# Laying out the output projection of seven heads as four rows per partition in a decode kernel

## The chip, the cores and the metric

The kernel runs on one core of a Trainium2 chip. The metric is the device time of one execution in microseconds; lower is better. Before and after were always timed in alternating rounds on the same chip.

Two numbers are given for every run: the *time* (the metric) and the *span*, which goes from the first instruction of the trace to the last.

## The reference, cut to what matters

One decode token passes through two branches that a sigmoid gate mixes. The attention branch has 16 query heads, 8 KV heads, 65536 cached positions and head size 256, so it reads 512 MiB of K and V. Its result goes through `wo`, 4096 x 448 in bf16 (3.67 MB).

```python
q = (x @ wq).reshape(B, Sq, 16, 256).transpose(0, 2, 1, 3)
k, v = repeat(k_cache, 2, axis=1), repeat(v_cache, 2, axis=1)
p = softmax(einsum("bhqd,bhkd->bhqk", q, k) * 256 ** -0.5)
o = einsum("bhqk,bhkd->bhqd", p, v)
a = o.transpose(0, 2, 1, 3).reshape(B, Sq, 16 * 256) @ wo      # wo: 4096 x 448
out = g * a + (1 - g) * b                                      # b: a small gated MLP
```

Of the kernel before, what the change touches and what calls it, by code (L numbers as in the profile page):

```python
# [12 lines left out]
ALU = AluOpType  # L13
# [11 lines left out]
class _Plan:  # L25
# [8 lines left out]
    def op(self, eng, key, fn, deps=()):  # L34
        o = _Op(eng, key, fn, deps)
        self.ops.append(o)
        return o

    def dma(self, eng, key, sem, fn, deps=()):
        if sem not in self.dsem:  # L40
            self.dsem[sem] = self.es.enter_context(self.nc.semaphore("d_" + sem))
        o = _Op(eng, key, fn, deps, dma=sem)
        self.ops.append(o)
        return o
# [75 lines left out]
def bass_gated_mix__gqa_block_cached__glu_gated_reglu__decode_kernel(  # L120
# [13 lines left out]
    H = A_k_cache.shape[1]  # L134
    S = A_k_cache.shape[2]
    DH = A_k_cache.shape[3]
    D = A_x.shape[2]
    F = B_W_gate.shape[1]
    NQ = A_wq.shape[1]
    J = 2 * H  # L140
# [15 lines left out]
    with es:  # L156
# [3 lines left out]
        ring = [sb("ring%d" % i, [128, U * DH], BF) for i in range(NRING)]  # L160
# [8 lines left out]
        o_sb = sb("o_sb", [128, 512], BF)  # L169
# [7 lines left out]
        emat = sb("emat", [128, 4], BF)  # L177
# [4 lines left out]
        X = sb("hs", [128, 20], F32)  # L182
        attnT = sb("attnT", [128, H * 4], BF)
# [32 lines left out]
        T_ps = M_ps[:, 480:484]  # L216
# [5 lines left out]
        op, dma = pl.op, pl.dma  # L222
        touch_m = []

        def mop(*a, **k):
            o = op(*a, **k)
            touch_m.append(o)
            return o
# [17 lines left out]
        t = 3.0  # L246
# [10 lines left out]
        slot, held, freed = {}, {2: ["gu", "dn"]}, {}  # L257
        r = 0
        for kind, i, _ in order:
            if kind in ("k", "v") or (kind, i) in (("wo", 0), ("vp", 0)):  # L260
# [3 lines left out]
                held[sl] = [(kind, i)]  # L264
                r += 1
        wo_sb = ring[slot["wo", 0]][:, 0:J * 2 * D].rearrange("p (j s n) -> p j s n", j=J, s=2)


        d_x = dma("ac", -9, "x", lambda e: e.dma_start(x_row, A_x[0, :, :]))
# [25 lines left out]
        g_em = op("gp", 0.4, lambda e: e.tensor_scalar(emat[:], iot1[:], 0.0, None, ALU.is_equal), [prev])  # L295
# [63 lines left out]
        def v_src(i):  # L359
            h, a = divmod(i, NTH)  # L360
            return A_v_cache[0, h, a * TK:(a + 1) * TK, :].rearrange("(m u) d -> m (u d)", u=U)
# [25 lines left out]
        def proj(e, lhsT, rhs, start, stop):  # L387
            for g in range(2):
                ins = e.matmul(A_ps[32 * g:32 * g + 1, 0:D2], lhsT, rhs[:, g * D2:(g + 1) * D2], start=start, stop=stop,  # L389
                               skip_group_check=True, tile_position=(0, 32 * g))  # L390
            return ins

        l_, qk, smax, aexp, pv, last = {}, {}, {}, {}, {}, {}
        pending = []

        def free(key):
            out_ = []
            for f in freed[key]:
                out_.append(l_[f] if isinstance(f, str) else qk[f[1], 1] if f[0] == "k" else pv[f[1]])
            return out_  # L400

        def make_pv(n, lo, hi, sl, tv, dep):
            h, a = divmod(n, NTH)

            def f_pv(e):
                for k in range(lo // 2, hi // 2):
                    g = k % 4
                    col = k * 16 + a
                    ins = e.matmul(OP[32 * g:32 * g + 4, :], ptp[:, col:col + 13:4],  # L409
                                   ring[sl][:, k * 512:(k + 1) * 512],  # L410
                                   start=(a == 0 and k < 4), stop=(a == NTH - 1 and k >= U // 2 - 4),
                                   tile_position=(0, 32 * g))
                return ins
            tp = max(tv, last["tev", h])
            deps = [dep] + last["ev", h] + ([last.get(("ocp", h - 1)), c_ps[2]] if a == 0 else [])
            pv[n] = op("pe", tp, f_pv, deps)
            if a == NTH - 1 and hi == U:
                tn = tp + (8.0 if n < NT - 1 else 1.2)
                o1 = op("dv", tn, lambda e: e.tensor_copy(o_sb[:], OP[:]), [pv[n], last.get(("otr", h - 1))])  # L419

                def f_otr(e):
                    for s in range(2):
                        for par in range(2):
                            ins = e.matmul(T_ps[:, 2 * s:2 * s + 2], o_sb[:, par * 256 + s:par * 256 + 256:2],  # L424
                                           emat[:, 2 * par:2 * par + 2], start=(par == 0), stop=(par == 1))
                    return ins
                o2 = mop("pe", tn + 0.5, f_otr, [o1, g_em])
                o3 = mop("dv", tn + 1, lambda e: e.tensor_tensor(
                    attnT[:, h * 4:(h + 1) * 4].rearrange("p (s q) -> p s q", q=2),
                    T_ps.rearrange("p (s q) -> p s q", q=2),  # L430
                    X[:, 8:10].unsqueeze(1).to_broadcast([128, 2, 2]), ALU.mult), [o2, last["rc", h]])
                last["ocp", h], last["otr", h], last["norm", h] = o1, o2, o3
                last["tn", h] = tn + 1

        for kind, i, t in issue:
# [43 lines left out]
            elif kind == "k":  # L479
                n = i  # L480
                h, t_ = divmod(n, NTH)
# [15 lines left out]
                if t_ == NTH - 1:  # L497
# [12 lines left out]
                    for rd in range(2):  # L510
# [10 lines left out]
                        p = op("pe", tt + 0.5, f_ptr, [rsc, g_idb, last.get(("bank", rd))])  # L521
# [7 lines left out]
                        q = op("ac", tt + 1, f_ev, [p, pv.get(h * NTH - 1)])  # L529
# [13 lines left out]
                    for args in [p_ for p_ in pending if p_[0] // NTH == h]:  # L543
                        make_pv(*args)
                        pending.remove(args)
            elif kind in ("v", "vp"):
                if kind == "v":
                    n, lo, hi = i, 0, U
                    sl = slot["v", n]
                    dep = dma("sp", t, "r%d" % sl, lambda e, sl=sl, n=n: e.dma_start(ring[sl][:], v_src(n)), free(("v", n)))  # L550
                else:
                    n, (lo, hi) = NT - 1, PIECES[i]
                    sl = slot["vp", 0]
                    dep = dma("sp", t, "vp%d" % i, lambda e, sl=sl, n=n, lo=lo, hi=hi: e.dma_start(  # L554
                        ring[sl][:, lo * 256:hi * 256], v_src(n)[:, lo * 256:hi * 256]), free(("vp", 0)))
                args = (n, lo, hi, sl, tL[kind, i], dep)
                if ("tev", n // NTH) in last:
                    make_pv(*args)
                else:
                    pending.append(args)  # L560
            elif kind == "wo":
                lo, hi = WO[i]
                l_["wo", i] = dma("sp", t, "wo%d" % i, lambda e, lo=lo, hi=hi: e.dma_start(
                    wo_sb[:, lo:hi, :, :], A_wo[lo * 256:hi * 256, :].rearrange("(j p s) n -> p j s n", p=128, s=2)), free(("wo", 0)))

        LAST = last["tn", H - 1]
        for i, (lo, hi) in enumerate(WO):
            for h in range(lo // 2, (hi + 1) // 2):
                key = max(tL["v", NT - 3] + 8, last["tn", h] + 0.5) + 0.01 * h
                if i in (1, 2):  # L570
                    key = LAST - (0.7, 0.2)[i - 1]
                elif i > 2:
                    key = LAST + 2 + 0.1 * i

                def f_wo(e, h=h, lo=max(lo, 2 * h), hi=min(hi, 2 * h + 2)):
                    for j in range(lo, hi):
                        for s in range(2):
                            c = h * 4 + s * 2 + j - 2 * h
                            ins = proj(e, attnT[:, c:c + 1], wo_sb[:, j, s, :], False, j == J - 1 and s == 1)
                    return ins  # L580
                fin = op("pe", key, f_wo, [l_["wo", i], last["norm", h], l_["dn"]])
        f0 = op("dv", T_END, lambda e: e.tensor_copy(fin_o[:, 0:D2], A_ps[0:1, 0:D2]), [fin])  # L582
        f1 = op("ac", T_END, lambda e: e.copy(fin_o[:, D2:D], A_ps[32:33, 0:D2]), [fin])
        f2 = dma("sp", T_END + 1, "out", lambda e: e.dma_start(out[0, :, :], fin_o), [f0, f1])
# [3 lines left out]
        pe = progs["pe"]  # L588
# [54 lines left out]
```

## The kernel before: what the change and the argument touch

All loads stand on one DMA queue. K and V come in tiles of 8 MiB (64 KiB per partition) into three ring buffers. The stream ends in this order: last K tile, V tile, first `wo` transfer (heads 0 to 4, 2240 KB), two V tiles (the second one in five pieces), then `wo` in four small transfers (448, 448, 224, 224 KB). These small ones fill the time in which the last V piece still has to be multiplied, copied and transposed.

```python
NW = H - 3
order += [("wo", 0, 7.3), ("v", NT - 3, TILE), ("v", NT - 2, TILE)]
PIECES = [(0, 64), (64, 96), (96, 112), (112, 120), (120, 128)]
...
WO = [(0, 2 * NW), (2 * NW, J - 4), (J - 4, J - 2), (J - 2, J - 1), (J - 1, J)]
```

A half head of `wo` (256 rows, index `j`) lies as two consecutive rows per partition, so every piece that a DMA moves is 2 x 448 x 2 = 1792 bytes. The attention output of a KV head (two query heads side by side in `o_sb`) must stand in the same order. Four small matmuls transpose it and one VectorE instruction scales it:

```python
def f_otr(e):
    for s in range(2):
        for par in range(2):
            ins = e.matmul(T_ps[:, 2 * s:2 * s + 2], o_sb[:, par * 256 + s:par * 256 + 256:2],
                           emat[:, 2 * par:2 * par + 2], start=(par == 0), stop=(par == 1))
    return ins
o2 = mop("pe", tn + 0.5, f_otr, [o1, g_em])
o3 = mop("dv", tn + 1, lambda e: e.tensor_tensor(attnT[...], T_ps..., X[:, 8:10]..., ALU.mult), ...)
...
l_["wo", i] = dma("sp", t, "wo%d" % i, lambda e, lo=lo, hi=hi: e.dma_start(
    wo_sb[:, lo:hi, :, :], A_wo[lo * 256:hi * 256, :].rearrange("(j p s) n -> p j s n", p=128, s=2)), free(("wo", 0)))
```

TensorE runs most of its program in a loop over the KV heads; what follows the loop (the last V tiles and the projection) is straight code.

## Time and profile before

| | before |
|---|---|
| time, median of 3 runs (range) | 1277.79 us (1277.51 to 1278.08) |
| span of the profiled run | 1276.2 us |
| DMA | 549.03 MB, mean 430 GB/s |
| TensorE / VectorE / ScalarE busy | 33% / 50% / 5% |

The DMA lines of the page show 40 equal slices of the span. The digit is the busy share in tenths, the second line the rate; the third counts packets by size:

```profile
DMA  9999999999999999999999999999999999999998
GB/s 398 443 433 430 435 429 438 435 431 429 435 433 440 428 429 435 433 440 429 431 435 431 438 431 433 435 431 432 438 431 431 435 431 438 433 429 435 415 444 348
DMA packets 12948, 549.22 MB, mean 430 GB/s; under 512 B 1283, under 2 KB 3590, under 8 KB 3974
```

No slice shows a pause. Between the first slice and the last, the slowest is the one with the small packets of the first `wo` transfer: it reads 415 GB/s. The last lines of the chain of waits (start, duration, what) show how the kernel ends:

```profile
1239.27 32.48 DMA ring<-in_A_wo_dram
1271.74 0.04 issue
1271.79 0.91 PE A_ps L389 x8
1272.70 0.20 PE M_ps L424 x4
1272.90 0.01 issue
1272.91 1.68 PE A_ps L389 x16
1274.59 0.02 issue
1274.61 0.38 DVE P_sb L582
```

TensorE waits until 1271.74 us for a `wo` transfer, then projects, transposes the last head (line 424) and projects the rest. The last four projections in turn wait for the last `wo` transfer, which lands at 1273.92 us, so this landing sets the end:

```profile
1273.96 0.15 PEld L389 LDWEIGHTS A_ps<-ring,attnT 128*1 128x1 bf16 x4 [0.22 <-DMA ring<-in_A_wo_dram]
```

Two issue lines matter as well. The first `wo` transfer was issued at 1173.78 us and landed 38.3 us later, at 1212.1 us. The V tile behind it was issued only at 1208.11 us, when the scores of the last K tile had freed its buffer:

```profile
ring<-in_A_wo_dram SPq DMA_DIRECT2D x1, 2240.0 KB, 38.3
```

```profile
1208.11 0.34 SPq L550 DMA_DIRECT2D ring<-in_A_v_cache_dram  x1
```

One more reading is needed, which no table of the profile shows. Each DMA is spread over 16 DMA engines, and its semaphore is raised once by each engine. The semaphore records of the trace therefore give 16 landing times for every transfer. For the first `wo` transfer they run from 1209.23 to 1212.10 us: the leading engine is 2.87 us ahead of the slowest. The transfer before it landed last at 1206.25 us, so the first `wo` transfer costs the slowest engine 5.85 us. "Lands" below means the last of the 16.

### The profile page before, as it was taken

How to read it: one execution, taken by the hardware profiler on the slowest of the kernel's cores; microseconds unless marked ns; L12 is line 12 of the kernel's file. 1: busy time of each engine (PE TensorE's matmuls, PEld its weight loads, DVE VectorE, ACT ScalarE, POOL GpSimd, SP SyncE). 2: the span in 40 equal slices, each digit the busy share in tenths (PEclk: the TensorE clock that was granted, in tenths of full speed). 3: DMA queues.
4: the chain of work that ended last, by engine and by line, in shares of the span. 5: the costliest groups of instructions: out<-in, count | busy, mean ns of one | idle time of the engine just before them, and what ended most of it. 6: DMA issues, size and time to landing. Idle time of an engine off the chain costs nothing. (4 is left out here: it accounts for less than half of the span.)

```text
span 1276.2 us, 10216 instructions
## 1 busy us (share of the span) xinstructions
PE 426.9 (33%) x4568; PEld 167.3 (13%) x4568; DVE 633.4 (50%) x421; ACT 63.3 (5%) x124; POOL 4.1 (0%) x21
## 2 busy tenths in 40 slices
PE   3633322334223431224331343321333313233255
PEld 1501110111001210002110111100111101011021
DVE  2698633465433655434555444555434655335600
ACT  0000000010000100001000010000100001000000
POOL 1000000000000000000000000000000000000000
PEclk9656666656666565666656666656666656666565
DMA  9999999999999999999999999999999999999998
GB/s 398 443 433 430 435 429 438 435 431 429 435 433 440 428 429 435 433 440 429 431 435 431 438 431 433 435 431 432 438 431 431 435 431 438 433 429 435 415 444 348
DMA packets 12948, 549.22 MB, mean 430 GB/s; under 512 B 1283, under 2 KB 3590, under 8 KB 3974
## 3 DMA queue, kind: packets, MB, share of 16 engines
q1 hardware_dynamic: 12930, 549.03, 99.7%
q8 instruction: 8, 0.13, 0.0%
q14 instruction: 6, 0.05, 0.0%
q10 hardware_dynamic: 4, 0.00, 0.0%
HBM read 549.03 MB, written 0.00 MB: 430 GB/s over the span
## 5 line engine op out<-in xcount | busy, mean ns | idle before, releaser
L367 DVE STREAM_TRANSPOSE ring<-ring 128x2048 uint32<-128x2048 uint32 x256 | 565.4, 2275 | 396.5 <-DMA ring<-in_A_k_cache_dram 396.5
L378 PE MATMUL ST<-ring,xc 128*16 128x512 bf16 x2048 | 223.9, 611 | 745.6 <-PEq L86 745.6
L378 PEld LDWEIGHTS ST<-ring,xc 128*16 128x16 bf16 x2048 | 68.3, 120 | 887.0 <-issue 886.1
L409 PE MATMUL O<-ring,ptp 128*4 128x512 bf16 x2048 | 150.7, 457 | 32.7 <-DMA ring<-in_A_v_cache_dram 18.7
L494 ACT ACTIVATE P_sb<-ST,nmb 128x512 bf16<-128x512 f32 x32 | 45.1, 1410 | 1102.2 <-DVE nmb L492 1102.2
L492 DVE TENSOR_REDUCE nmb<-ST 128x1 f32<-128x512 f32 x32 | 22.0, 689 | 116.8 <-PE ST L378 116.8
L409 PEld LDWEIGHTS O<-ring,ptp 128*4 128x4 bf16 x2048 | 56.4, 99 | 126.6 <-issue 69.3
L419 DVE CAST o_sb<-O 128x512 bf16<-128x512 f32 x8 | 5.5, 691 | 78.6 <-PE O L409 78.6
L513 DVE TENSOR_TENSOR P_sb<-P_sb,hs 128x1024 bf16<-128x1024 bf16 x16 | 18.9, 1221 | 9.4 <-ACT hs L507 9.4
L518 PE MATMUL PT<-identb,P_sb 128*128 128x128 bf16 x128 | 16.2, 307 | 16.8 <-PEq L86 15.8
L459 PE MATMUL M_ps<-xT,ring 128*128 128x1 bf16 x84 | 9.5, 205 | 17.2 <-DMA ring<-in_B_W_up_dram 17.2
L518 PEld LDWEIGHTS PT<-identb,P_sb 128*128 128x128 bf16 x128 | 12.4, 138 | 19.2 <-issue 19.2
L527 ACT COPY ptp<-PT 128x256 bf16<-128x256 bf16 x32 | 10.3, 375 | 23.9 <-PE PT L518 23.9
L341 PE MATMUL QN<-ring,P_sb 128*128 128x512 bf16 x32 | 8.9, 448 | 3.1 <-DMA ring<-in_A_wq_dram 3.1
L459 PEld LDWEIGHTS M_ps<-xT,ring 128*128 128x128 bf16 x84 | 7.2, 152 | 17.8 <-issue 17.4
L494 ACT ACTIVATION_READ_ACCUMULATOR P_sb<-ST,nmb 128x1 f32 x32 | 8.4, 262 | 0.0
L462 PE MATMUL M_ps<-xT,ring 128*64 128x1 bf16 x56 | 7.8, 276 | 0.0
L442 DVE STREAM_TRANSPOSE scr<-P_sb 128x256 uint32<-128x256 uint32 x1 | 0.4, 445 | 12.5 <-ACT P_sb L441 12.5
L503 PE MATMUL M_ps<-identf,hs 128*2 128x128 f32 x8 | 2.5, 308 | 11.1 <-PEq L86 11.1
L539 DVE RECIPROCAL hs<-M_ps 128x2 f32<-128x2 f32 x8 | 1.4, 170 | 8.3 <-PE M_ps L538 8.3
L462 PEld LDWEIGHTS M_ps<-xT,ring 128*64 128x64 bf16 x56 | 5.4, 191 | 0.4
L389 PE MATMUL A_ps<-ring,attnT 128*1 128x224 bf16 x64 | 4.6, 306 | 0.7 <-DMA ring<-in_A_wo_dram 0.6
(74 smaller groups left out, 65.7 us busy)
## 6 DMA issues: line engine op xcount, KB each, us to landing
ring<-in_A_v_cache_dram SPq DMA_DIRECT2D x1, 4096.0 KB, 23.6
ring<-in_A_wq_dram SPq DMA_DIRECT2D x1, 3072.0 KB, 10.5
ring<-in_A_wo_dram SPq DMA_DIRECT2D x1, 2240.0 KB, 38.3
ring<-in_A_v_cache_dram SPq DMA_DIRECT2D x1, 2048.0 KB, 28.2
ring<-in_B_W_down_dram SPq DMA_DIRECT2D x1, 1568.0 KB, 21.7
ring<-in_B_W_gate_dram SPq DMA_DIRECT2D x1, 1344.0 KB, 32.9
ring<-in_B_W_up_dram SPq DMA_DIRECT2D x1, 1344.0 KB, 35.5
ring<-in_A_v_cache_dram SPq DMA_DIRECT2D x1, 1024.0 KB, 30.2
```

The source lines that it names most:

```text
L341: ins = e.matmul(QN_ps, xw3[:, k_, 31 - h:159 - h], rhs, start=(h == 0 and kt == 0), stop=(h == H - 1 and kt == R3))
L367: return lambda e: e.transpose(v, v)
L378: ins = e.matmul(bank[32 * w:32 * w + 16, :], xc[:, x0:x0 + 16], ktv[sl][:, u0:u0 + 16, c, :, r_], start=(b == 0 and c == 0 and r_ == 0), ...
L409: ins = e.matmul(OP[32 * g:32 * g + 4, :], ptp[:, col:col + 13:4], ring[sl][:, k * 512:(k + 1) * 512], start=(a == 0 and k < 4), stop=(a = ...
L419: o1 = op("dv", tn, lambda e: e.tensor_copy(o_sb[:], OP[:]), [pv[n], last.get(("otr", h - 1))])
L459: e.matmul(GU_ps[:, c:c + 1], wf3[which][:, kt * F + ft:(kt + 1) * F:FT], xT[:, kt:kt + 1], start=(kt == 0), stop=False, skip_group_check= ...
L462: ins = e.matmul(GU_ps[64 * half:64 * half + 64, c:c + 1], wfh[which][:, ft:F // 2:FT], xT[:, R3 + half:R3 + half + 1], start=False, stop= ...
L492: smax[n] = op("dv", tk + 22, lambda e, n=n, NM=NM, t_=t_: e.tensor_reduce(NM[:, t_:t_ + 1], ST[n % 2][:], AX.X, ALU.max, negate=True), [q ...
L494: aexp[n] = op("ac", tk + 23, lambda e, n=n, t_=t_, NM=NM, RS=RS: e.activation(P_sb[:, t_:2048:4], ST[n % 2][:], ACTF.Exp, bias=NM[:, t_:t ...
L513: rsc = op("dv", tt, lambda e, X=X, pb=pb: e.tensor_tensor(pb, pb, X[:, 12:16].unsqueeze(1).to_broadcast([128, 256, 4]), ALU.mult), [h7, a ...
L518: ins = e.transpose(PT[rd][:, s * 128:(s + 1) * 128], P_sb[:, (rd * 8 + s) * 128:(rd * 8 + s + 1) * 128], identb[:, :])
L527: ins = e.copy(dst, src)
```

## The change: intent and diff

The intent is to halve the number of DMA pieces of `wo` without moving more bytes: four rows per partition make pieces of 3584 B. A whole KV head (512 rows) then is one piece per partition. Head 7 is left alone, because it comes in halves at the very end. In exchange the transposition needs 16 smaller matmuls per head instead of four, and the scaling two VectorE instructions instead of one.

```diff
+        wo4 = ring[slot["wo", 0]][:, 0:J * 2 * D].rearrange("p (h s n) -> p h s n", h=H, s=4)
...
+                def f_otr4(e):
+                    for s in range(4):
+                        for q in range(2):
+                            for par in range(2):
+                                ins = e.matmul(T_ps[64 * q:64 * q + 64, s:s + 1], o_sb[:, par * 256 + s:par * 256 + 256:4],
+                                               emat[:, 2 * par + q:2 * par + q + 1], start=(par == 0), stop=(par == 1),
+                                               skip_group_check=True)
+                    return ins
+
+                def f_norm4(e):
+                    for q in range(2):
+                        ins = e.tensor_scalar(attnT[64 * q:64 * q + 64, h * 4:(h + 1) * 4], T_ps[64 * q:64 * q + 64, :],
+                                              X[64 * q:64 * q + 64, 8 + q:9 + q], None, ALU.mult)
+                    return ins
...                                                        # both for h < H - 1
+                if hi <= J - 2:
+                    dst, src = wo4[:, lo // 2:hi // 2, :, :], A_wo[lo * 256:hi * 256, :].rearrange("(h p s) n -> p h s n", p=128, s=4)
+                else:
+                    dst, src = wo_sb[:, lo:hi, :, :], A_wo[lo * 256:hi * 256, :].rearrange("(j p s) n -> p j s n", p=128, s=2)
...                                                        # and f_wo4, the projection from the new order
```

More of the change, by code (lines that the diff above doesn't have):

```diff
@@ L426, in f_otr @@
                     return ins
-                o2 = mop("pe", tn + 0.5, f_otr, [o1, g_em])
-                o3 = mop("dv", tn + 1, lambda e: e.tensor_tensor(
+                def f_otr4(e):
[11 more added lines that the diff above has]
+                    return ins
+                o2 = mop("pe", tn + 0.5, f_otr if h == H - 1 else f_otr4, [o1, g_em])
+                o3 = mop("dv", tn + 1, f_norm4 if h < H - 1 else lambda e: e.tensor_tensor(
                     attnT[:, h * 4:(h + 1) * 4].rearrange("p (s q) -> p s q", q=2),
@@ L562, in bass_gated_mix__gqa_block_cached__glu_gated_reglu__decode_kernel @@
                 lo, hi = WO[i]
-                l_["wo", i] = dma("sp", t, "wo%d" % i, lambda e, lo=lo, hi=hi: e.dma_start(
-                    wo_sb[:, lo:hi, :, :], A_wo[lo * 256:hi * 256, :].rearrange("(j p s) n -> p j s n", p=128, s=2)), free(("wo", 0)))
+                if hi <= J - 2:
+                    dst, src = wo4[:, lo // 2:hi // 2, :, :], A_wo[lo * 256:hi * 256, :].rearrange("(h p s) n -> p h s n", p=128, s=4)
+                else:
+                    dst, src = wo_sb[:, lo:hi, :, :], A_wo[lo * 256:hi * 256, :].rearrange("(j p s) n -> p j s n", p=128, s=2)
+                l_["wo", i] = dma("sp", t, "wo%d" % i, lambda e, dst=dst, src=src: e.dma_start(dst, src), free(("wo", 0)))
         LAST = last["tn", H - 1]
@@ L573, in bass_gated_mix__gqa_block_cached__glu_gated_reglu__decode_kernel, with f_wo4 @@
                     key = LAST + 2 + 0.1 * i
+                def f_wo4(e, h=h):
+                    for s in range(4):
+                        ins = proj(e, attnT[:, h * 4 + s:h * 4 + s + 1], wo4[:, h, s, :], False, False)
+                    return ins
                 def f_wo(e, h=h, lo=max(lo, 2 * h), hi=min(hi, 2 * h + 2)):
@@ L580, in f_wo @@
                     return ins
-                fin = op("pe", key, f_wo, [l_["wo", i], last["norm", h], l_["dn"]])
+                fin = op("pe", key, f_wo4 if h < H - 1 else f_wo, [l_["wo", i], last["norm", h], l_["dn"]])
         f0 = op("dv", T_END, lambda e: e.tensor_copy(fin_o[:, 0:D2], A_ps[0:1, 0:D2]), [fin])
```

## The prediction

> **What bounds the kernel now.** The DMA stream: on the page's DMA lines nearly every slice reads 9 tenths, mean 430 GB/s over 549.03 MB, while TensorE is busy 33% and VectorE 50%. The chain of waits ends with 32.48 us of the `wo` transfer, then 0.91 us of projections, 0.20 us of transposes, 1.68 us of projections and a 0.38 us copy. Time can come only from a shorter stream, on its slowest DMA engine, or from the 3.5 us after it.
>
> **What the change moves.** The bytes stay. The `wo` rows of heads 0 to 6 come as 896 pieces of 3584 B instead of 1792 of 1792 B. In the trace's packet records a 1792 B packet of `wo` takes 78 ns (mean; 74 undisturbed), 4096 B 160 ns, 65536 B 2423 ns. At the large packets' rate (27.06 B/ns) 1792 B need 66 ns: 8 to 12 ns per packet. But packets overlap: the 80 packets per engine of the first `wo` transfer land 5.85 us after the tile before (slowest engine), 73 ns each. The Trainium skill, "DMA: Bandwidth & Descriptors", section "Why small descriptors are slow (HBM only)", names a fixed cost of about 3 cycles per packet; the trace agrees in kind, with some 7 ns. Scaled from 4096 B, 3584 B take 139 to 140 ns (estimate), so a pair saves 7 to 9 ns (15 if mean durations added up). Each of 16 engines loses 40 + 8 + 8 packets: 0.3 us in the first transfer, 0.15 us in the two 448 KB ones; estimate 0.45 us, at most 0.9.
>
> **How much is critical.** The V tiles behind the first `wo` transfer are issued at 1208.1 us, after the last K tile's scores, not after `wo`. The engine that finishes `wo` first (1209.2 us) already runs dry for about 0.75 us; the slowest (1212.1 us) does not. The leaders will only wait longer; the slowest, which ends the kernel, keeps its saving. Instruction fetches (16 KB, about 0.6 us of one engine) delay single engines, so another may become last and cap that part near 0.3 us. In the tail the last two half-head pieces and head 7's transposition are untouched, and the last matmuls wait for the last landing: the end follows it.
>
> **What is added.** 12 more matmuls per head for seven heads (about 1.2 us of TensorE per 155 us) and one VectorE instruction of 0.16 us. Head 6's transposition stands at 1174.3 us with 21 us of idle TensorE behind it; K and V transfers are issued 33 to 51 us before landing against 19.35 us of transfer. None of it reaches the end.
>
> **Prediction.** 1277.3 us, 0.5 us (0.04%) less; 1276.6 to 1278.0 in 8 of 10. Runs of before spread by 0.57 us, so the gain is at the edge of what can be measured. Within 2%: 0.985; faster 0.005; slower 0.01.
>
> **What would show it.** Packets under 2 KB fall from 3590 to about 1800, all packets by 896, MB unchanged. The first `wo` transfer's last landing comes 5.5 us after the tile before, not 5.85; the end 0.3 to 0.6 us earlier. The `emat` transposes grow from 32 to 116 matmuls. The V issue stays near 1208.1 us.
>
> **What would make it wrong.** A 3584 B packet costing as much as two of 1792 B; the longer TensorE loop body being fetched again each round, which would delay one DMA engine by 0.6 us each time; fetches falling on the slowest engine; the added transposes holding a ring buffer, which issue times would show.

## The result and the profile after

| | before | after |
|---|---|---|
| time, median of 6 runs (range) | 1277.65 us (1277.39 to 1278.08) | 1277.95 us (1277.70 to 1278.16) |
| ratio, 95% interval | | 1.0002 (0.9989 to 1.0015) |
| span of the profiled run | 1276.2 us | 1276.2 us |

A ratio here is the mean time of one kernel's runs over that of the other's of the same rounds, so not quite the ratio of the medians quoted. The predicted half microsecond of gain is absent.

The DMA lines of the page of after. The slice of the first `wo` transfer reads 411 GB/s, no better, because such slices mix V and `wo`:

```profile
DMA  9999999999999999999999999999999999999998
GB/s 397 443 433 430 429 438 433 438 431 429 435 433 438 430 431 433 435 435 431 431 433 435 433 435 429 431 440 428 440 431 431 435 431 435 435 429 433 411 449 350
DMA packets 12052, 549.22 MB, mean 430 GB/s; under 512 B 1283, under 2 KB 1798, under 8 KB 3078
```

There are 896 packets fewer, as intended. From 1271.7 us on the chain of waits ends as before, each step within 0.03 us:

```profile
1239.42 32.33 DMA ring<-in_A_wo_dram
1271.76 0.04 issue
1271.80 0.91 PE A_ps L390 x8
1272.71 0.20 PE M_ps L425 x4
1272.91 1.66 PE A_ps L390 x16
1274.57 0.02 issue
1274.59 0.38 DVE P_sb L605
```

The wait for the last `wo` transfer ends at the same time too (it lands at 1273.95 us, before 1273.92):

```profile
1273.99 0.10 PEld L390 LDWEIGHTS A_ps<-ring,attnT 128*1 128x1 bf16 x4 [0.27 <-DMA ring<-in_A_wo_dram]
```

The issue lines of after: the first `wo` transfer is issued at 1174.07 us and lands 37.7 us later; the V tile behind it is still issued at 1208.3 us.

```profile
ring<-in_A_wo_dram SPq DMA_DIRECT2D x1, 2240.0 KB, 37.7
```

```profile
1208.32 0.34 SPq L565 DMA_DIRECT2D ring<-in_A_v_cache_dram  x1
```

The added work, in the group lines of after (112 new matmuls, 14 new VectorE instructions; before had 32 matmuls and 8 instructions of this kind):

```profile
L432 PE MATMUL M_ps<-emat,o_sb 128*64 128x1 bf16 x112 | 4.5, 199 | 6.6 <-PEq L86 6.6
L439 DVE TENSOR_SCALAR attnT<-M_ps,hs 64x4 bf16<-64x4 f32 x14 | 3.1, 220 | 6.3 <-PE M_ps L432 6.2
```

Read with the landing records, the gain is there and then disappears. The table follows the slowest landing from the last K tile on:

| step, last landing to last landing (us) | before | after |
|---|---|---|
| first `wo` transfer (2240 KB) | 5.85 | 5.54 |
| first V tile behind it | 19.37 | 19.36 |
| second V tile behind it (the last full one) | 19.37 | 19.61 |
| first `wo` piece of the tail (448 KB) | 1.19 | 1.37 |
| last K tile to end of `wo`, in all | 87.03 | 87.14 |

The first transfer saves 0.31 us. A V tile whose layout did not change gives back 0.24 us of it, and the first tail piece, which should have become 0.1 us cheaper, costs 0.18 us more. So the loss is not in `wo` as such, and the question is what happens in these two places.

### The profile page after: what moved, and what is told of

It reads as the page before. It is cut to its first block, busy times and chain, and to the rows that moved or that the text cites. A ratio compares the mean times of both kernels' runs of the same rounds, so it can differ in the third digit from the quotient of the medians.

```text
span 1276.2 us, 10391 instructions
## 1 busy us (share of the span) xinstructions
PE 432.4 (34%) x4652; PEld 171.5 (13%) x4652; DVE 635.3 (50%) x428; ACT 63.3 (5%) x124; POOL 4.1 (0%) x21
## 2 busy tenths in 40 slices
DMA packets 12052, 549.22 MB, mean 430 GB/s; under 512 B 1283, under 2 KB 1798, under 8 KB 3078
## 5 line engine op out<-in xcount | busy, mean ns | idle before, releaser
L432 PE MATMUL M_ps<-emat,o_sb 128*64 128x1 bf16 x112 | 4.5, 199 | 6.6 <-PEq L86 6.6
L439 DVE TENSOR_SCALAR attnT<-M_ps,hs 64x4 bf16<-64x4 f32 x14 | 3.1, 220 | 6.3 <-PE M_ps L432 6.2
## 6 DMA issues: line engine op xcount, KB each, us to landing
ring<-in_A_wo_dram SPq DMA_DIRECT2D x1, 2240.0 KB, 37.7
```

## The theory and its rivals

The trace records one other kind of DMA traffic: instruction fetches. Queue 8 fetches 16 KiB at a time, eight times in either kernel. The Trainium skill, "Runtime: NRT & Kernel Launch", section "Instruction fetch mechanics", says that instruction memory is refilled in blocks of 16 KiB, 256 instructions, and that crossing a boundary is mostly hidden. The trace agrees on the size for queue 8 (packets of 16384 B); the packets of the second instruction queue, 14, have 8192 B. Six of queue 8's fetches come before 110 us, two come in the last 40 us.

Here are the DMA queue lines from 1238 to 1245 us, first for before and then for after (queue, packets, MB, share of 16 engines). Both kernels have a fetch on queue 8 and one on queue 14:

```profile
q1 hardware_dynamic: 47, 3.08, 102.7%
q8 instruction: 1, 0.02, 0.8%
q14 instruction: 1, 0.01, 0.3%
```

```profile
q1 hardware_dynamic: 46, 3.01, 100.9%
q8 instruction: 1, 0.02, 0.8%
q14 instruction: 1, 0.01, 0.3%
```

And the same lines from 1268 to 1271 us. Before has no fetch there (its last one comes at 1271.96 us), after has it, at 1269.13 us:

```profile
q1 hardware_dynamic: 607, 1.16, 104.5%
```

```profile
q1 hardware_dynamic: 391, 1.20, 100.0%
q8 instruction: 1, 0.02, 2.0%
```

**The theory.** A fetch of queue 8 takes 0.93 to 1.10 us in the records (a data packet of the same size takes 0.61 us) and delays the one DMA engine that serves it. Behind the first `wo` transfer the leading engines have run dry and wait for the V tile issued at 1208.1 us; they restart together, only 2.1 us (before) or 1.7 us (after) ahead of the slowest. In before a fetch that hits one of them stays hidden behind the slowest engine. In after the slowest engine is 0.3 us earlier, so an engine hit at 1241 us becomes the last one. Then the last fetch, which comes earlier because TensorE's program is 24 instructions longer, hits the stream once more.

**Rival A.** Fewer packets are worth nothing to the end of the stream. **Rival B.** The added matmuls and VectorE instructions cost the gain by themselves.

## The experiments

Twelve kernels ran, each with 4 or 5 counted runs. Two of them give a wrong result.

### Only the layout: the old transposition with the new `wo`

```diff
-                o2 = mop("pe", tn + 0.5, f_otr if h == H - 1 else f_otr4, [o1, g_em])
-                o3 = mop("dv", tn + 1, f_norm4 if h < H - 1 else lambda e: e.tensor_tensor(
+                o2 = mop("pe", tn + 0.5, f_otr, [o1, g_em])
+                o3 = mop("dv", tn + 1, lambda e: e.tensor_tensor(
```

> The new wo layout with the old four-matmul transposition (wrong result on purpose), so TensorE's program is as long as before's. Theory (the gain is real but instruction fetches take it back): the first wo transfer lands 5.53 us after the tile before it, as in after; the last instruction fetch comes at about 1272 us again, not at 1269; the first tail piece of wo is no longer held back (1.05 to 1.1 us after the piece before, not 1.37), so the last wo landing is 0.2 to 0.3 us earlier than in before or after (1273.65 to 1273.75 against 1273.92 and 1273.95); time 0.2 to 0.3 us under before. Rival A (smaller packet count is worth nothing at the end): equal to before within 0.1 us. Rival B (the added matmuls and VectorE work cost the gain): the same 0.3 to 0.5 us gain as the theory, so B is told apart by the third run, not this one.

Measured: 1277.63 us median, against 1277.65 us for before (ratio 0.9998, 0.9985 to 1.0012). The result is wrong. The first transfer takes 5.54 us, the last fetch comes at 1272.05 us and the first tail piece takes 1.17 us. The first two parts were as expected, and the tail piece was no longer held back, though 1.05 to 1.1 us had been expected. The rest of the expectation failed: the last landing came at 1274.47 us instead of 1273.65 to 1273.75, and the time did not fall by 0.2 to 0.3 us. The second V tile took 20.00 us, 0.64 us too long, with the fetch at 1242.3 us in it. In this trace, of the slowest of the five runs, the first place alone swallowed the whole gain.

### Only the longer TensorE program

```diff
+                def f_otr_more(e):
+                    for i in range(12):
+                        e.matmul(M_ps[64 * (i % 2):64 * (i % 2) + 64, 484 + i // 2:485 + i // 2], o_sb[:, i // 2:i // 2 + 256:4],
+                                 emat[:, i % 4:i % 4 + 1], start=True, stop=True, skip_group_check=True)
+                    return f_otr(e)
-                o2 = mop("pe", tn + 0.5, f_otr, [o1, g_em])
+                o2 = mop("pe", tn + 0.5, f_otr if h == H - 1 else f_otr_more, [o1, g_em])
```

> Before, with 12 more small matmuls per head for heads 0 to 6 (right result, their output is unused), so TensorE's program grows by the same 24 instructions as in after, without the new layout. Theory: the last instruction fetch moves from 1271.96 to about 1269.1 us; the engine it hits ends near the slowest, so the end moves by 0 to 0.2 us only[...]. Rival B (added work costs time by itself): 0.3 to 0.5 us slower than before, with unchanged fetch time.

Measured: 1277.75 us median (1277.33 to 1278.58). The queue lines from 1268 to 1271 us of this kernel show the fetch, as in after:

```profile
q1 hardware_dynamic: 507, 1.16, 99.6%
q8 instruction: 1, 0.02, 2.3%
```

It came at 1269.71 us, and the first tail piece took 1.60 us instead of 1.19. So 24 more instructions alone move the fetch and hold that piece back, with before's layout. The second V tile took 19.38 us: hidden, as the theory says. From the last K tile to the end of `wo` there were 87.43 us, 0.40 more than in before, where 0 to 0.2 had been expected. The profiled run was the slowest of five; a time difference to before is not resolved.

### After, with TensorE's program back at before's length

```diff
-                            for half in range(2):
+                            for half in range(1 if which == 0 and ft < 12 else 2):
```

> After with 12 matmuls (24 instructions) of the gate projection at the start left out (wrong result on purpose), so TensorE's program has before's length while the 16-matmul transpositions stay. Theory: last fetch back at about 1272 us, last wo landing 0.2 to 0.3 us earlier than after's 1273.95, time 0.2 to 0.3 us under after. Rival B: same time and same last landing as after.

Measured: 1277.77 us median (1277.65 to 1278.04), wrong result. The same queue lines have no fetch any more:

```profile
q1 hardware_dynamic: 380, 1.21, 101.4%
```

It came at 1271.44 us, and the first tail piece took 1.13 us. The stream from the last K tile to the end of `wo` took 87.02 us, 0.12 us less than in after, half of what I expected; the second V tile still took 19.66 us. The last landing itself, at 1273.99 us, was not earlier than after's 1273.95, as I had expected; here the last 224 KB piece took 0.68 us instead of 0.56, with the fetch at 1271.44 us shortly before it. The time is lower than after's by 0.18 us in the median, inside the spread. Rival B expected the same last landing and the same time as after, so by these two numbers the run does not count against it; only the fetch and the first tail piece moved as the theory says.

### Smaller pieces: 896 B

```diff
-                    wo_sb[:, lo:hi, :, :], A_wo[...].rearrange("(j p s) n -> p j s n", p=128, s=2)), ...
+                    wo_sb[:, lo:hi, :, :], A_wo[...].rearrange("(j s p) n -> p j s n" if hi <= J - 2 else "(j p s) n -> p j s n", p=128, s=2)), ...
```

(The transposition of heads 0 to 6 reads `o_sb` in blocks of 128 instead of every second element, so the result is right.)

> Before with wo of heads 0 to 6 in pieces of 896 B, one row each (right result). Both theories that believe in a fixed cost per packet: 896 B packets about 40 ns, first wo transfer 6.4 to 6.6 us after the tile before (80 more packets per engine at 7 to 9 ns), the two 448 KB pieces about 0.13 us longer each; here the slowest engine carries all of it, so the end is 0.7 to 1.0 us later than before. Rival A (packet count does not matter at the end): within 0.1 us of before.

Measured: 1277.91 us median (1277.49 to 1278.13; ratio 1.0001). My expectation failed. Packets of 896 B are recorded with 41 ns, but they overlap so well that the first transfer took 5.87 us with 160 packets per engine, against 5.85 us with 80. No cost per packet shows in the landings between 896 and 1792 B.

### The disputed cost made three times as large

The first `wo` transfer is issued three times, with the copies in unused space of its buffer. No engine runs dry behind it any more: in tripled before the leading engine stays 2.90 to 2.93 us ahead of the slowest from the first `wo` transfer through the V tiles. `sA` is the source in 3584 B pieces; the other kernels use 1792, 896 or 17920 B for the copies.

```diff
+                if i == 0:
+                    for c in (1, 2):
+                        o = J * 2 * D + (c - 1) * 20 * D
+                        dst = ring[slot["wo", 0]][:, o:o + 20 * D].rearrange("p (j m) -> p j m", j=5)
+                        l_["wox", c] = dma("sp", t + 0.001 * c, "wox%d" % c, lambda e, dst=dst, src=sA: e.dma_start(dst, src), free(("wo", 0)))
```

> Before with the first wo transfer (2240 KB in 1792 B pieces) issued three times, the two copies into unused space of the same buffer (right result). Makes the disputed cost three times as large, and keeps the leading DMA engines from running dry behind it. Expected by all theories: two more transfers of 5.85 us on the slowest engine, 11.5 to 11.8 us slower than before.

> After with the first wo transfer (2240 KB in 3584 B pieces) issued three times in the same way (right result). Theory (the saving of about 0.31 us per transfer is real, and in the plain kernels is hidden by which DMA engine ends last): 0.7 to 1.2 us faster than the tripled before. Rival (the landing times mislead, larger pieces are worth nothing to the end of the stream): equal to the tripled before within 0.2 us.

> The tripled before, with the two copies in 896 B pieces. The 896 B run showed 5.87 us for the first transfer, the same as 1792 B, against my theory of a fixed cost per packet (6.4 to 6.6 us). If that reading holds: equal to the tripled before within 0.3 us. If a fixed cost per packet exists after all: 1.1 to 1.4 us slower.

> The tripled before, with each of the two copies as one 17920 B piece per partition. If large pieces run at the K and V tiles' 434 GB/s, a copy takes 5.3 us: 1.0 to 1.2 us faster than the tripled before. If 3584 B is already the end of the gain (5.54 us): 0.6 us faster.

| kernel | pieces of the copies | one copy lands after (us) | second V tile (us) | time, median (us) |
|---|---|---|---|---|
| tripled before | 1792 B | 6.02 | 19.35 | 1289.55 (1289.49 to 1289.78) |
| tripled before | 896 B | 6.0 | 19.35 | 1289.47 (1289.46 to 1289.68) |
| tripled after | 3584 B | 5.64 | 19.36 | 1288.86 (1288.52 to 1289.12) |
| tripled before | 17920 B | 5.35 | 19.36 | 1288.19 (1288.13 to 1288.21) |

The packet lines from 1212.5 to 1217.5 us, where nothing but copies moves, for 1792, 896, 3584 and 17920 B, one kernel each:

```profile
DMA packets 1075, 1.90 MB, mean 380 GB/s; under 512 B 15, under 2 KB 1075, under 8 KB 1075
```

```profile
DMA packets 2110, 1.88 MB, mean 375 GB/s; under 512 B 15, under 2 KB 2110, under 8 KB 2110
```

```profile
DMA packets 584, 2.04 MB, mean 407 GB/s; under 512 B 16, under 2 KB 16, under 8 KB 584
```

```profile
DMA packets 135, 2.13 MB, mean 427 GB/s; under 512 B 16, under 2 KB 16, under 8 KB 16
```

Of the expectations, the one for 896 B held (0.08 us apart) and the one for tripled after was just missed (0.69 us faster, 0.7 to 1.2 expected). Tripled before was 11.97 us slower than before instead of 11.5 to 11.8, because a copy takes 6.02 and not 5.85 us, and 17920 B gained 1.36 us instead of 1.0 to 1.2.

Three points follow. Rival A falls: with a tripled transfer the new layout shortens the kernel by 0.69 us (the ranges do not overlap), and its span by 1.1 us in the mean; what the two differ by is explained below. The step is between 1792 and 3584 B (380 to 407 GB/s), not below it, and 17920 B gains another 0.29 us per transfer. And the second V tile takes 19.35 to 19.36 us in all four, although the same two fetches fall into it (at 1253 to 1257 us here): where no engine has run dry, the leaders have up to 2.9 us in hand, which is enough to hide them.

### Moving bytes from the tail into the dry time

If the theory holds, head 5's 448 KB should stand in the first `wo` transfer, where the leaders wait anyway. Both layouts got this edit (the planned times of the transfers and of the projections, which went with it, are left out):

```diff
-        WO = [(0, 2 * NW), (2 * NW, J - 4), (J - 4, J - 2), (J - 2, J - 1), (J - 1, J)]
-        for i in range(1, 5):
+        WO = [(0, J - 4), (J - 4, J - 2), (J - 2, J - 1), (J - 1, J)]
+        for i in range(1, 4):
```

> After, with head 5's 448 KB of wo taken into the first wo transfer instead of the tail (right result, meant as the version that beats both). Theory (in after two paths end together: the slowest engine, which gained, and the engines that ran dry until the V tiles issued at 1208.1 us, then were hit by an instruction fetch, which did not): moving 1.07 us of stream into the dry time takes the second path 1.1 us back, so the slowest engine's gain shows: last wo landing 1273.3 to 1273.6 us (before 1273.92, after 1273.95), time 0.3 to 0.5 us under before and after. Rival A (the end of the stream is not shortened by larger pieces): equal to its partner with before's layout.

> Before with the same move and its own layout (right result): the control. Theory: the slowest engine carries the same bytes in the same pieces, so the last landing stays within 0.15 us of 1273.92 and the time within 0.2 us of before; its partner is 0.3 to 0.5 us faster. If the move itself were the gain, both would gain the same.

Measured: 1278.06 us (1278.02 to 1278.53) with the new layout and 1278.08 us (1278.04 to 1278.33) with the old, both slower than before's 1277.51 us of the same rounds. The landing part came out in the main: the second V tile took 19.36 us in both, and from the last K tile to the end of `wo` there were 86.62 us with the new layout, 87.15 us with the old (before: 87.03). The stream kept its gain of 0.53 us against the control. The last landings, 1273.73 and 1274.14 us, both came later than expected (1273.3 to 1273.6, and within 0.15 us of 1273.92). The time did not follow (0.3 to 0.5 us less than before was expected with the new layout, no change beyond 0.2 us with the old; both were some 0.55 us slower), because I had mis-sized the tail. The chain of waits of the new layout, moved:

```profile
1240.88 30.71 DMA ring<-in_A_v_cache_dram
1271.59 0.04 issue
1271.63 0.63 PE O L409 x4
1272.26 0.02 issue
1272.28 0.70 DVE o_sb L419
1272.98 0.05 issue
1273.03 0.27 PE M_ps L424 x4
1273.29 1.61 PE A_ps L389 x9
```

The end now hangs on the last V piece, which lands one transfer later: multiply, copy, transpose, project. The 448 KB in the tail had covered exactly this chain. So this was no version that beats both, and none was found.

### Before and after again

> Before unchanged, for the spread: the time within 0.3 us of 1277.65. Theory: the lag of the slowest DMA engine differs by 0.1 to 0.3 us from run to run, the last instruction fetch again near 1272 us.

> After unchanged: time 1277.7 to 1278.1; the first wo transfer lands 5.53 us after the tile before, the last instruction fetch again near 1269 us, the slowest engine within 0.3 us of two others at the end.

Measured: before 1277.66 us, after 1277.80 us (1277.79 to 1278.35). The repeated traces agree with the first ones: first transfer 5.85 and 5.49 us, second V tile 19.36 and 19.54 us, last fetch at 1272.21 and 1269.46 us, first tail piece 1.19 and 1.70 us. At the end the slowest engine of after was 0.6 us behind the next one, not within 0.3 us as I expected.

### What the runs have in common

| kernel | `wo` pieces | TensorE program | first `wo` | second V tile | last fetch at | first tail piece | last K to end of `wo` |
|---|---|---|---|---|---|---|---|
| before / again | 1792 B | as before | 5.85 / 5.85 | 19.37 / 19.36 | 1272.0 / 1272.2 | 1.19 / 1.19 | 87.03 / 87.05 |
| longer program | 1792 B | +24 | 5.82 | 19.38 | 1269.7 | 1.60 | 87.43 |
| 896 B | 896 B | as before | 5.87 | 19.37 | 1272.2 | 1.20 | 87.10 |
| after / again | 3584 B | +24 | 5.54 / 5.49 | 19.61 / 19.54 | 1269.1 / 1269.5 | 1.37 / 1.70 | 87.14 / 87.35 |
| only the layout | 3584 B | as before | 5.54 | 20.00 | 1272.1 | 1.17 | 87.25 |
| after, shortened | 3584 B | as before | 5.55 | 19.66 | 1271.4 | 1.13 | 87.02 |

In this table the second V tile is late in every trace with 3584 B pieces and in none with smaller ones; the first tail piece is late in every trace with 24 more instructions and in none without. (Tripled after and after moved have both and show neither; the first tail piece takes 1.10 and 1.08 us in them. In the one the leaders have 2.9 us in hand, in the other the last fetch comes already at 1265.54 us.)

The packet records do not name the DMA engine that serves a fetch, but the 16 landings of a transfer show that single engines fall back. In tripled before, the distances of the engines to the slowest repeat from one K or V tile to the next within 0.02 us, until the V tile with the two fetches: there two of the sixteen change, from 2.80 and about 2.91 us ahead to 1.48 and 2.08. In after moved the last fetch of queue 8 comes alone, at 1265.54 us, and in the next landing one engine is 0.28 us ahead that was about 1.84 us ahead before it. And where the table shows a second V tile that is late by 0.25, 0.18, 0.64 and 0.30 us, the distance from the slowest engine to the next is 0.22, 0.14, 0.61 and 0.28 us, while it was 0.65 to 0.96 us a tile earlier: a new engine has fallen behind the old slowest by about the delay.

### A part of the time that no busy table shows

Every run has both a time and a span, and their difference separates the kernels without overlap. It is 1.25 to 1.46 us in all runs of before, of only the layout, of the longer TensorE program, of 896 B, of the moved control and of the three tripled kernels built on before. It is 1.61 to 1.80 us in all runs of the five kernels that have the new transposition and scaling: after, after again, after shortened, after moved and after tripled.

The semaphore records show the place. After the last instruction, one semaphore is raised nine times in a closing sequence. Eight gaps lie between them. In all nine traces of the first group they are, to within 1 ns (ns, before):

```
34  39  44  23   98  39  34  47
```

and in all five of the second, equally closely (ns, after):

```
34  38  44  23  454  39  34  46
```

One step takes 454 instead of 98 ns, always the same one. The Trainium skill, "Runtime: NRT & Kernel Launch", section "The ~15µs preamble/postamble breakdown", gives about 355 ns, eight hops of 44 ns, for a semaphore that five engines pass on in the barrier in front of the kernel, and lists a barrier behind it without a time per hop. The eight gaps of before, behind the kernel, sum to 358 ns, so the mean agrees, while single gaps range from 23 to 98 ns. So one step comes 0.36 us late, after the kernel's own end; the records do not name its engine.

Neither the layout nor the longer TensorE program does it: the kernels with one of these alone have 98 ns. What is left is the pair that the five kernels share, the 16-matmul transposition and the two-instruction scaling. In the metric, then, rival B is partly right: taking out the pair alone (only the layout) takes out the 0.36 us, which are not part of its execution. The traces hold one more trait of these five kernels. A fetch of 8 KiB on queue 14 comes at 417.6 to 417.9 us in them, and at 439.3 to 440.1 us in the nine others. A longer TensorE program alone does not move it and a shortened one does not move it back, so it fits the VectorE program, which is 7 instructions longer in the five. That this is also what delays the closing step is not shown: no kernel separates it, and it stays open.

## Why the prediction was right or wrong

The measured 1277.95 us lies inside the stated range, and "within 2%" was right, but the gain of 0.5 us did not come. That the number fell into the range says little: the range reached up to 1278.0 us and so held before's own 1277.65 us as well. In the mean of all runs after is 0.28 us slower (1277.92 us of 11 runs against 1277.64 us of 32 runs of before, each with a spread of 0.2 us as standard deviation). Of the spans of the same runs, after's are 0.11 us shorter, which is inside that spread; 0.40 us more lie outside the span. So of the 0.8 us between the predicted and the measured difference, about half is gain lost inside the span and half is time added behind it.

- *The DMA stream bounds the kernel.* Right: two more transfers of 6.02 us made it 11.97 us longer.
- *The first `wo` transfer lands 5.5 us after the tile before.* Right: 5.54 and 5.49 us. The packet counts (1798 under 2 KB, 896 fewer in all), 116 matmuls of the `emat` kind and the V issue near 1208.1 us (1208.3) came out too.
- *A pair saves 7 to 9 ns because of a fixed cost per packet.* The size was right (0.31 us over 40 pairs is 8 ns; in step, 0.38 us is 9.5 ns). The reason was not borne out: 896 B pieces cost no more per byte than 1792 B ones. Which property of the 3584 B piece helps stays open.
- *"The slowest, which ends the kernel, keeps its saving ... the end follows it."* This is the step that failed. The caution behind it, that "another may become last", named the mechanism, but I took it for a cap near 0.3 us. The slowest engine did keep its saving, but it no longer ended the stream: in the four plain traces with 3584 B pieces another engine came in behind it, and the second V tile was 0.18 to 0.64 us late, against a saving of 0.30 to 0.36 us in the first transfer.
- *"The longer TensorE loop body being fetched again each round"*: did not happen, eight fetches in either kernel. What I missed is that a program of other length moves the place of its last fetch. 24 instructions moved it by some 2.5 us into the stream, which held the first tail piece back by 0.2 to 0.6 us.
- *"None of it reaches the end"*, of the added instructions: right for their execution, in the span. Outside it, 0.36 us appear in the closing sequence of every kernel with the new transposition and scaling. The profile's page does not show this; the time against the span does.

## What to carry to other kernels

When a stream bounds a kernel, ask which of the 16 DMA engines ends last, and how far behind it the next ones are: a saving on the slowest engine is worth no more than that distance. A change of a few instructions can also move instruction fetches (here 24 instructions moved one by some 2.5 us), and in these traces fetches set single DMA engines back among the data. So a gain of some tenths of a microsecond should be tested by making its cause several times larger, as the tripled transfer did. Compare the time with the span as well as the spans with each other, because work can be lost behind the last instruction.

## What the Trainium skill lacked or had wrong

- "DMA: Bandwidth & Descriptors", section "Why small descriptors are slow (HBM only)", gives a fixed cost of about 3 cycles per packet. The landings do not show it between 896 and 1792 B (one copy of 2240 KB lands after 6.0 us with both), while 3584 B takes 5.64 us and 17920 B 5.35 us.
- "Runtime: NRT & Kernel Launch", section "Instruction fetch mechanics", calls the cost of a block boundary mostly hidden. No run here measured that for the engine that executes. The data stream did notice: with a fetch of 16 KiB just before it, a 448 KB transfer near the end took 1.37, 1.60 and 1.70 us in three traces, against 1.13 to 1.20 us in five traces without.
- The same page, section "The ~15µs preamble/postamble breakdown", gives eight hops of 44 ns for the barrier in front of the kernel and no hop for the one behind it. There the eight gaps sum to 358 ns in before and to 712 ns in after: one step takes 98 ns in nine kernels and 454 ns in five. No page says what makes a step long.
